# Half tiles of a routed MLP behind pooled attention: split weights fetched from DRAM, choices made earlier, and a new table of issue times

## The chip, the cores and the metric

The kernel runs on one core of a Trainium2 chip. The metric is the time of one execution on the device in microseconds (us). Before the change the median of three runs is 2346.57 us (2337.69 to 2347.06).

The names used below: PE is the matrix engine (TensorE), ACT the scalar engine, DVE the vector engine, POOL the GpSimd engine, SP the engine whose queue issues most of the transfers. PSUM is the memory that PE writes its sums into, in eight banks.

## The reference

Two stages follow each other. The first is attention in which keys and values are one and the same: `kv` (4 batches of 384 x 32 x 128) is averaged over 4 x 4 blocks, which leaves 768 rows a batch, and multiplied by `w_sr`. Each of the 12288 queries of a batch is scored against them, and the softmax of the scores weighs them.

```python
kv_pool = kv.reshape(B, H // r, r, W // r, r, C).mean(axis=(2, 4))
kv_flat = kv_pool.reshape(B, -1, C) @ w_sr          # keys = values, 768 x 128 a batch
s = scale * (q @ k.transpose(0, 2, 1)); s = s - s.max(-1, keepdims=True)
a = np.exp(s); a /= a.sum(-1, keepdims=True) + 1e-09
x = (a @ v)                                         # 49152 rows of 128
```

The second stage sends each of the 49152 rows to the one of eight experts whose gate logit is largest, runs that expert's two-layer MLP (128 to 1024 to 128, ReLU between) and scales the result by the gate's probability.

```python
expert_idx = np.argmax(x @ w_gate, axis=1)
for e in range(E):
    h = np.maximum(x[mask] @ w1[e], 0.0)
    out[mask] = gate_w[mask, None] * (h @ w2[e])
```

## The kernel before

**Work per tile.** Queries go through in 96 tiles of 512. Every product is made of three matmuls on split numbers: an operand is kept as a high part (a rounding copy, made by ACT) and a low part (the difference, made by POOL or DVE), and `mm3` (L230) adds high x high, high x low and low x high. For a tile of attention, PE computes scores in four groups of 128 queries (`scores`), DVE takes the maxima, ACT the exponentials (`exps`), DVE turns 32 x 32 blocks (`turn_p`), SP moves the blocks with 16 transfers (`move_p`), ACT and POOL split the result in three pieces (`high_p`, `low_p`), and PE multiplies by the values in six steps (`values` 0 to 5, where 0 and 1 read the piece that POOL makes second).

**Routing.** `route` turns the result (`turn_x`, the X matmuls of L500), finds each row's expert and its place among that expert's rows (`places`, L579), and POOL writes the rows into the DRAM buffer `xs` with four indirect transfers (`put`, L595). Before a tile's rows are written, POOL clears the row buffer (`norm`, the memset of L486).

**Expert tiles.** Once an expert has 512 rows, they can be taken. `choose` (L659) picks an expert with a chain of small DVE operations on eight numbers, SP loads the choice into registers (`where`), fetches that expert's split weights from `ws` into one of two buffers (`fetch`, L753, only if the buffer does not hold them yet; 2 MB), and loads the rows (`read`, L723). `experts` then turns the rows (`turn_m`), splits them (`high_m` on ACT, `low_m` on POOL, tile name `xl`), and runs eight pairs of steps: `first(f)` (xh, xl against the first weights), `high_h` on ACT, `low_h` on DVE (tile `hlow`), `second(f)`, which comes a good two steps after its `first`. `turn_y`, `rows_y` (tile `yo`) and POOL's four indirect transfers to the output (`put`, L860) end the tile.

**The end.** 94 expert tiles are of 512 rows. Then at most a few rows are left with each expert, and half tiles of 256 take them: six always (tiles 94 to 99), more behind a branch, which the data here does not take. A half tile before the change loads its expert's unsplit weights (1 MB) into the attention buffers `pb` and `pt` (`fetch_whole`, L759) and splits them in four pieces each with ACT, POOL and DVE (`cut`, L768) into the two weight buffers. Its row numbers `tok` (L805, L809) sit in a pool of three buffers, so that a new one waits until the output transfers of three tiles earlier have landed.

**What sets the order.** Nothing runs in loops: every step is entered into a plan with a time (`at`, L52) and the plan is emitted in order of these times. The times come from the table `AT` (L32), in units of which a tile of 512 has 16. For PE, ACT and DVE the order of emission is the order of issue; POOL and SP take theirs from it too. Each engine works its list off in that order. So a change of numbers in `AT` moves instructions past each other on every engine, and nothing else about them.

**Three further facts used below.** Each batch's keys are pooled by DVE (`pool`, L261) during earlier tiles: three batches of six blocks, so 18 tiles carry an extra reduction. The results of `first` sit in three PSUM banks (`take`, `give`, L180 to L187), so a `first` waits until `low_h` has freed a bank. The scores use one pair of banks in turn.

Of the kernel before, what the change touches and what calls it, by code (L numbers as in the profile page):

```python
# [29 lines left out]


AT = {  # L32
    "turn_q": -0.15, "high_q": 3.34, "low_q": 5.01, "maxima": 1.13, "exps": 2.45, ("first_p", 0): 5.48,
    ("first_p", 1): 4.1, ("first_p", 2): 4.74, ("first_p", 3): 5.1, ("first_p", 4): 5.32,
    ("first_p", 5): 7.4, "first_high": 0.5, "first_low": 1.3, "first_values": 2.69, "turn_p": 2.65,
    "move_p": 17.32, ("high_p", 0): 28.78, ("high_p", 1): 25.01, ("high_p", 2): 29.02, "low_p": 0.45,
    ("values", 0): 37.6, ("values", 1): 38.01, ("values", 2): 39.41, ("values", 3): 39.91,
    ("values", 4): 41.61, ("values", 5): 42.21, "copy_x": 0.6, "turn_x": 1.76, "logits": 0.8, "row": 1.7,
    "gate_exp": 2.27, "gate": 2.29, "ranks": 1.12, "places": 2.13, "put_x": 3.83, "expert": 24.43,
    "fetch": -12.69, "read": -9.0, "weights": -5.6, ("cut", 0, 0): -7.93, ("cut", 1, 0): 3.67,  # L40
    ("cut", 0, 1): 1.14, ("cut", 1, 1): 3.1, "turn_m": -4.57, "high_m": 1.58, "low_m": 2.94, "first": 4.6,
    "high_h": 0.0, "low_h": 1.35, "second": 4.85, "copy_y": 0.52, "pads": 4.0, "split": -14.0, "splits": 11.0, "turn_y": 1.61, "rows_y": 4.66,
}


# [17 lines left out]
def tile_pooled_attention_top1_moe(ctx: ExitStack, tc, q, kv, w_sr, w_gate, w1, w2, out):  # L63
# [154 lines left out]
    def low(dst, src, h, eng=nc.vector):  # L218
        eng.tensor_tensor(out=dst, in0=src, in1=h.bitcast(F32), op=ALU.subtract)  # L219

    def load_turned(name, rows, n):

        blocks = ap.tile([P, T], F32, name=name)
        bv = blocks[:, :n].rearrange("p (t c) -> p t c", c=SQ)
        return blocks, [
            nc.sync.dma_start(out=bv[cs], in_=rows[:, cs].rearrange("(t r) c -> r t c", r=SQ)).ins  # L226
            for cs in (slice(k, k + SQ) for k in range(0, P, SQ))
        ]
# [430 lines left out]
    def choose(j):  # L659
# [26 lines left out]
        if final:  # L686

            less = table("less", E)
            nc.vector.tensor_scalar(
                out=less, in0=rem, scalar1=-1.0, scalar2=float(n), op0=ALU.mult, op1=ALU.add  # L690
            )
            nc.vector.scalar_tensor_tensor(out=less, in0=less, scalar=0.0, in1=pick, op0=ALU.max, op1=ALU.mult)
            nc.vector.tensor_tensor(out=pks[:, 0], in0=pks[:, 0], in1=less, op=ALU.subtract)
            thr = rp.tile([P, 1], F32, name="thr" + tag, bufs=4)
# [28 lines left out]
    def read(j):  # L723
        own = state["tile", j]
        rows = xs[bass.ds(own["row"], size(j)), :]
        own["xb"], gets = load_turned("xb", rows, size(j))
        own["tokf"] = rp.tile([P, G], F32, name="tokf", bufs=3)
        tokf = own["tokf"][:, : size(j) // P]
        gets.append(nc.sync.dma_start(out=tokf, in_=rows[:, P].rearrange("(g p) -> p g", p=P)).ins)
        assert state["sent"] >= min(j + AHEAD, NS - 1)  # L730
        for get in gets:
            for put in state["puts"]:
                tc.add_manual_dep(
                    get, put.name,
                    mybir.DependencyInfo(mybir.DependencyClass.Sync, mybir.DependencyReason.DATA),
                    reason="the rows are there",
                )
            tc.add_to_no_dep_group("rows", get)
        state["puts"] = []

    def weights(t, j):
# [14 lines left out]
                out=wt.bitcast(F32), in_=ws[bass.ds(own["ex"], 1)].rearrange("o p n f -> p (o n) f"), cond=own["new"]  # L756
            )

        def fetch_whole():  # L759
            for n in range(2):  # L760
                own[n] = ap.tile([P, F], F32, name=("pb", "pt")[n])
            nc.sync.dma_start(out=own[0], in_=w1[bass.ds(own["ex"], 1)].rearrange("o p f -> p (o f)"))
            nc.sync.dma_start(
                out=own[1].rearrange("p (f d) -> p f d", d=D),
                in_=w2[bass.ds(own["ex"], 1)].rearrange("o (f p) d -> p (o f) d", p=P),
            )
# [6 lines left out]
        at(t + AT["fetch"], where)  # L773
        if j < FULL:
            at(t + AT["weights"], fetch)
            return
        at(t + AT["fetch"], fetch_whole)
        for n in range(2):
            for c in range(F // T):
                at(t + AT["cut", n, c], cut, n, c)  # L780

    def experts(t, j):
        own = {}
        wt = wts[j % 2]
        n = size(j)
        per = T // n

# [9 lines left out]
        def low_m():  # L797
            own["xl"] = mp.tile([P, T], F32R, name="xl")[:, :n]
            low(own["xl"], own["xt"], own["xh"], nc.gpsimd)
            gs = slice(0, n // P)  # L800
            tok = own["tok"] = rp.tile([P, G], I32, name="tok", bufs=3)
            if own["thr"] is None:
                nc.gpsimd.tensor_copy(out=tok[:, gs], in_=own["tokf"][:, gs])
            else:
                old = rp.tile([P, G], F32, name="old")  # L805
                nc.vector.tensor_scalar(
                    out=old[:, gs], in0=slot[:, gs], scalar1=own["thr"], scalar2=BIG, op0=ALU.is_lt, op1=ALU.mult
                )
                nc.vector.tensor_tensor(out=tok[:, gs], in0=old[:, gs], in1=own["tokf"][:, gs], op=ALU.add)  # L809

        def first(f):
            if state.pop("head", False):
                scores_in(0)
                free.append(5)
            hp = own["hp", f] = take()
            for k in range(per):
                fs = slice((f * per + k) * P, (f * per + k + 1) * P)
                mm3(hp[:, k * n : (k + 1) * n], wt[:, 0, fs], wt[:, 1, fs], own["xh"], own["xl"], True, True)
# [12 lines left out]

        def second(f):
            y = own["y"] = ps[:, BANK_Y, :n]
            for k in range(per):
                fb, ns = f * per + k, slice(k * n, (k + 1) * n)
                fs = slice(fb * D, (fb + 1) * D)
                mm3(
                    y, wt[:, 2, fs], wt[:, 3, fs], own["hh", f][:, ns], own["hl", f][:, ns],
                    fb == 0, fb == FB - 1,
                )  # L840

# [44 lines left out]
    def tiles(i, u):  # L886

        if i >= AHEAD:
            tile_j(i - AHEAD, u)

    def tile_j(j, u=None):
        t = 16 * (min(j, FULL) + AHEAD + 3) + 8 * max(j - FULL, 0) + AT["expert"]
# [55 lines left out]
```

## Time and profile before

| | us |
|---|---|
| median of three runs | 2346.57 |
| the profiled execution | 2344.68 |
| its span in the trace | 2343.0 |
| PE busy | 2179.0 (93% of the span) |
| POOL busy | 1832.5 (78%) |
| DVE busy | 1777.1 (76%) |
| ACT busy | 1494.3 (64%) |

The span is what the trace covers, first to last instruction; 1.7 us of the execution lie outside it. The granted clock of PE is its full 2.4 GHz for nearly the whole span, and lower in the first 200 us and in the last 80. PE's busy time counts matmuls that overlap in its pipeline. POOL's busy time leaves out the 0.3 us between two indirect transfers, so its 78% understates how full its queue is. The time line has three parts: a start of about 200 us in which the attention runs ahead, a long steady part in which one attention tile and one expert tile go through together, and an end of about 120 us with expert tiles alone.

### The profile page before, as it was taken

To read this page: it belongs to the slowest core of one execution; us is meant where nothing else is said; L and a number is where in the kernel's file an instruction comes from. 1 tells how busy PE (TensorE), PEld (TensorE's weight loads), DVE (VectorE), ACT (ScalarE), POOL (GpSimd) and SP (SyncE) were. 2 spreads that over 40 slices of the span, in tenths; PEclk is the share of its full clock that TensorE was granted. 3 is DMA by queue.
4 is the path that set the end of the run, shared out by engine and by line. 5 is a ranking of instruction groups with operands and counts; after the bars stand their busy time and mean duration, and the time that the engine had idled before them with its cause. 6 is when DMAs were issued, how large, how long until landed. Compare 5 with 4: busy or idle time off the path is not lost.

```text
span 2343.0 us, 41042 instructions
## 1 busy us (share of the span) xinstructions
PE 2179.0 (93%) x10630; PEld 1788.3 (76%) x10630; DVE 1777.1 (76%) x4368; ACT 1494.3 (64%) x3031; POOL 1832.5 (78%) x1957
## 2 busy tenths in 40 slices
PE   6778999999999999999999999999998999999986
PEld 6667877778777787778877777777786878788765
DVE  2566878987777778987786778998776777877564
ACT  2656666666666676666666666666665666666553
POOL 2656888878887888878887888878887888888863
PEclk9999999999999999999999999999999999999997
DMA  8866556655565556655556556665556555554341
GB/s 237 282 191 148 124 133 157 161 122 116 121 156 145 125 116 157 160 139 117 119 143 159 127 119 147 163 146 123 113 151 143 128 119 119 127 119 112 89 116 53
DMA packets 590357, 324.59 MB, mean 139 GB/s; under 512 B 497048, under 2 KB 515609, under 8 KB 588064
## 3 DMA queue, kind: packets, MB, share of 16 engines
q1 hardware_dynamic: 565408, 268.34, 51.0%
q0 software_dynamic: 24704, 53.53, 6.6%
q8 instruction: 87, 1.43, 0.3%
q14 instruction: 158, 1.29, 0.2%
HBM read 287.84 MB, written 72.88 MB: 154 GB/s over the span
## 4 chain that ended last, share of the span: by engine, by line
POOL 31%; PE 21%; DMA 13%; issue 13%; DVE 9%; SPq 8%; ACT 3%; POOLq 0%; DVEq 0%; ACTq 0%
POOL pt L219 18%; PE ps L231 7%; PE ps L232 6%; DMA xs<-row,dst 6%; PE ps L233 6%; POOL out_dram L860 5%; DMA xb<-xs 5%; POOL xs L595 4%; SPq L382 4%; SPq L226 3%; DVE hlow L826 3%; ACT prob L362 2%; POOL pos L586 1%; PE ps L500 1%; DVE pb L371 1%
## 5 line engine op out<-in xcount | busy, mean ns | idle before, releaser
L822 ACT ACTIVATE hh<-ps 128x512 fp32r<-128x512 f32 x776 | 465.3, 600 | 323.4 <-PE ps L233 309.8
L826 DVE SCALAR_TENSOR_TENSOR hlow<-ps,hh 128x512 fp32r<-128x512 f32 x776 | 529.1, 682 | 179.7 <-ACT hh L822 177.8
L219 POOL TENSOR_TENSOR pt<-pt,pth 128x1024 fp32r<-128x1024 f32 x270 | 640.4, 2413 | 2.8 <-ACT pth L216 1.8
L362 ACT ACTIVATE prob<-ps,nmax 128x768 f32<-128x768 f32 x384 | 346.2, 902 | 265.4 <-DVE nmax L354 265.2
L860 POOL DMA_INDIRECT out_dram<-yo,tok x388 | 384.8, 992 | 130.1 <-issue 79.9
L595 POOL DMA_INDIRECT xs<-row,dst x384 | 380.1, 990 | 116.1 <-issue 89.4
L371 DVE STREAM_TRANSPOSE pb<-prob 128x768 f32<-128x768 f32 x360 | 352.1, 978 | 88.5 <-ACT prob L362 78.6
L231 PE MATMUL ps<-xh,wt 128*128 128x512 f32 (+1 forms) x800 | 340.3, 425 | 75.2 <-DVE hlow L826 64.3
L354 DVE TENSOR_REDUCE nmax<-ps 128x1 f32<-128x768 f32 x384 | 364.7, 950 | 51.2 <-PE ps L233 49.9
L231 PE MATMUL ps<-hh,wt 128*128 128x512 f32 (+1 forms) x800 | 323.2, 404 | 0.0
L216 ACT CAST pth<-pt 128x1024 fp32r<-128x1024 f32 x270 | 273.4, 1047 | 69.6 <-DMA pt<-pb 55.2
L232 PE MATMUL ps<-hlow,wt 128*128 128x512 f32 (+1 forms) x800 | 314.1, 393 | 2.7 <-DVE hlow L826 2.7
L232 PE MATMUL ps<-xl,wt 128*128 128x512 f32 (+1 forms) x800 | 314.1, 393 | 1.5 <-POOL xl L219 1.5
L233 PE MATMUL ps<-xh,wt 128*128 128x512 f32 (+1 forms) x800 | 313.7, 392 | 0.0
L233 PE MATMUL ps<-hh,wt 128*128 128x512 f32 (+1 forms) x800 | 312.1, 390 | 0.0
L231 PE MATMUL ps<-kh,qh 128*128 128x384 f32 x768 | 269.7, 351 | 4.6 <-ACT qh L216 2.3
L232 PE MATMUL ps<-kl,qh 128*128 128x384 f32 x768 | 260.4, 339 | 0.0
L233 PE MATMUL ps<-kh,ql 128*128 128x384 f32 x768 | 259.6, 338 | 0.8 <-POOL ql L219 0.8
L231 PEld LDWEIGHTS ps<-xh,wt 128*128 128x128 f32 x800 | 153.4, 192 | 118.2 <-DVE hlow L826 95.1
L232 PE MATMUL ps<-pt,vh 128*128 128x512 f32 x540 | 213.8, 396 | 3.4 <-POOL pt L219 3.4
L231 PE MATMUL ps<-pth,vh 128*128 128x512 f32 x540 | 214.6, 397 | 0.0
L233 PE MATMUL ps<-pth,vl 128*128 128x512 f32 x540 | 213.8, 396 | 0.0
(133 smaller groups left out, 3824.6 us busy)
## 6 DMA issues: line engine op xcount, KB each, us to landing
wt<-ws SPq DMA_DIRECT2D x94, 2048.0 KB
pt<-pb SPq DMA_DIRECT2D x1440, 96.0 KB
raw<-in_kv_dram SPq DMA_DIRECT2D x96, 256.0 KB
qb<-in_q_dram SPq DMA_DIRECT2D x384, 64.0 KB
xb<-xs SPq DMA_DIRECT2D x376, 64.0 KB
ws<-wt SPq DMA_DIRECT2D x8, 2048.0 KB
raw<-in_moe_w_dram SPq DMA_DIRECT2D x16, 512.0 KB
out_dram<-yo,tok POOLq DMA_INDIRECT x388, 2.3
```

The source lines that it names most:

```text
L216: nc.scalar.copy(out=dst, in_=src)
L219: eng.tensor_tensor(out=dst, in0=src, in1=h.bitcast(F32), op=ALU.subtract)
L231: nc.tensor.matmul(out=ps, lhsT=wh, rhs=xh, start=start, stop=False)
L232: nc.tensor.matmul(out=ps, lhsT=wh, rhs=xl, start=False, stop=False)
L233: nc.tensor.matmul(out=ps, lhsT=wl, rhs=xh, start=False, stop=stop)
L354: nc.vector.tensor_reduce(out=nmax, in_=own["s", g][:, :, :NH], op=ALU.max, axis=AX.XY, negate=True)
L362: nc.scalar.activation(out=prob.rearrange("p (h k) -> p h k", h=2), in_=own["s", g][:, :, :NH], func=AF.Exp, bias=own["nmax", g], scale=1. ...
L371: nc.vector.transpose(out=own["pb"][:, :, :, g, :].rearrange("p c b t -> p b c t"), in_=own["prob", g].rearrange("p (b c t) -> p b c t", c ...
L595: put = nc.gpsimd.indirect_dma_start(out=xs, out_offset=bass.IndirectOffsetOnAxis(ap=dst[:, g : g + 1].bitcast(U32), axis=0), in_=own["row ...
L822: nc.scalar.activation(out=hh, in_=own["hp", f], func=AF.Relu)
L826: nc.vector.scalar_tensor_tensor(out=hl, in0=own["hp", f], scalar=0.0, in1=own["hh", f].bitcast(F32), op0=ALU.max, op1=ALU.subtract,)
L860: put = nc.gpsimd.indirect_dma_start(out=out, out_offset=bass.IndirectOffsetOnAxis(ap=own["tok"][:, g : g + 1].bitcast(U32), axis=0), in_= ...
```

## The change

Five things change.

1. The half tiles take the split weights from `ws`, 2 MB each, without a condition and in two transfers of 1 MB. The fetches go into four sets of buffers in turn: two sets are the buffers of `pb` and `pt`, two are the weight buffers of the full tiles. `cut` and its splits are gone.
2. The half tiles' rows go into buffers of the names `raw` and `prob`, which the attention no longer needs by then.
3. The choices of the experts for tiles 94 to 99 are planned one after the other, 4.6 units apart, right behind that of tile 93; before, each was planned 6 units ahead of its `where`.
4. The pools of `tok`, `tokf` and `thr` get eight buffers and that of `num` four; `old` moves to PSUM.
5. The table `AT` has other numbers in some 30 entries, so that the order on every engine is another.

```diff
-    "turn_q": -0.15, "high_q": 3.34, "low_q": 5.01, ...
+    "turn_q": 0.06, "high_q": 3.87, "low_q": 5.01, ...
...
-    def load_turned(name, rows, n):
-        blocks = ap.tile([P, T], F32, name=name)
+    def load_turned(name, rows, n, pool=ap):
+        blocks = pool.tile([P, T], F32, name=name, bufs=3 if name in ("raw", "prob") else 2)
...
-        num = rp.tile([P, 3], I32, name="num" + tag)
+        num = rp.tile([P, 3], I32, name="num" + tag, bufs=4)
...
-        own["xb"], gets = load_turned("xb", rows, size(j))
-        own["tokf"] = rp.tile([P, G], F32, name="tokf", bufs=3)
+        k = (j - FULL) % 6
+        own["xb"], gets = load_turned(*(("xb", rows, size(j)) if j < FULL else
+                                        ("raw", rows, size(j), kp) if k < 3 else ("prob", rows, size(j))))
+        own["tokf"] = rp.tile([P, G], F32, name="tokf", bufs=8)
...
-        def fetch_whole():
-            for n in range(2):
-                own[n] = ap.tile([P, F], F32, name=("pb", "pt")[n])
-            nc.sync.dma_start(out=own[0], in_=w1[bass.ds(own["ex"], 1)].rearrange("o p f -> p (o f)"))
...
-        def cut(n, c):
-            cs = slice(c * T, (c + 1) * T)
-            high(wt[:, 2 * n, cs], own[n][:, cs])
-            low(wt[:, 2 * n + 1, cs], own[n][:, cs], wt[:, 2 * n, cs], nc.vector if c else nc.gpsimd)
+        def fetch_end():
+            k = (j - FULL) % 4
+            if k < 2:
+                w1p = ap.tile([P, 2, F], F32, name="pb").bitcast(F32R)
+                w2p = ap.tile([P, 2, F], F32R, name="pt")
+            else:
+                w1p, w2p = wts[j % 2][:, :2], wts[j % 2][:, 2:]
+            own["wt"] = (w1p, w2p)
+            for n, w in enumerate(own["wt"]):
+                nc.sync.dma_start(
+                    out=w.bitcast(F32),
+                    in_=ws[bass.ds(own["ex"], 1)].rearrange("o p n f -> p (o n) f")[:, 2 * n : 2 * n + 2],
+                )
...
+        u = start(j - 4) + (size(j - 4) // 32 - 2) + AT["first"] + AT["second"] + 0.1
+        u = t + AT["fetch_end"] if j < FULL + 2 else max(t + AT["fetch_end"], u)
+        at(t + AT["fetch_end"], where)
+        at(u, fetch_end)
...
-            tok = own["tok"] = rp.tile([P, G], I32, name="tok", bufs=3)
+            tok = own["tok"] = rp.tile([P, G], I32, name="tok", bufs=8)
...
-                old = rp.tile([P, G], F32, name="old")
+                old = table("old", G)
...
-        if ("tile", j) not in state:
-            select(t + AT["fetch"] - 6 if u is None else u, j)
+        t = start(j)
+        if j < SURE:
+            state["chosen"] = state["chosen"] + 4.6 if u is None else u
+        if j != SURE:
+            select(state["chosen"] if j < SURE else t + AT["fetch_end"] - 6, j)
         weights(t, j)
-        at(t + AT["read"], read, j)
+        at(t + AT["read"] if j < FULL else t + AT["fetch_end"] + 0.1, read, j)
```

What the new table does to the order is seen at three places. The first is POOL's queue over one period of the steady part. Names: `pt` and `pth` are the pieces of `low_p`, `pos` and `dst` the places, `xs` the routed rows, `out_dram` the output, `row` the buffer that the memset clears. Before:

```order
L860 DMA out_dram<-yo,tok 49152x128 x4
L219 TENSOR_TENSOR pt<-pt,pth 128x4x256 x3
L586 TENSOR_TENSOR pos<-pos,oh 128x8 x3
L587 TENSOR_TENSOR pos<-pos,oh 128x32
L219 TENSOR_TENSOR ql<-qt,qh 128x512
L803 CAST tok<-tokf 128x4
L595 DMA xs<-row,dst 397312x144 x4
L219 TENSOR_TENSOR xl<-xt,xh 128x512
L486 MEMSET row 128x4x15
L487 TENSOR_SCALAR row<-slot 128x4
```

POOL's queue in the same period, after the change:

```order
L219 TENSOR_TENSOR pt<-pt,pth 128x4x256 x3
L586 TENSOR_TENSOR pos<-pos,oh 128x8 x3
L587 TENSOR_TENSOR pos<-pos,oh 128x32
L219 TENSOR_TENSOR ql<-qt,qh 128x512
L595 DMA xs<-row,dst 397312x144 x4
L868 DMA out_dram<-yo,tok 49152x128 x4
L219 TENSOR_TENSOR xl<-xt,xh 128x512
L809 CAST tok<-tokf 128x4
L486 MEMSET row 128x4x15
L487 TENSOR_SCALAR row<-slot 128x4
```

The four output transfers have moved from behind the memset to right behind the four row transfers, ahead of `xl` and of the memset.

The second place is PE in the same part, from the turning of a finished expert tile (`ident,yt`) on. `xh` marks a `first`, `hh` a `second`, `vh` a step of `values`, `kh,qh` scores. Before:

```order
L849 MATMUL ps<-ident,yt 128x128 x4
L231 MATMUL ps<-xh,wt_109 128x512
L232 MATMUL ps<-xl,wt_109 128x512
L233 MATMUL ps<-xh,wt_109 128x512
L273 MATMUL ps<-ident,pooled 128x128
L231 MATMUL ps<-hh,wt_109 128x512
L232 MATMUL ps<-hlow,wt_109 128x512
L233 MATMUL ps<-hh,wt_109 128x512
L231 MATMUL ps<-kh,qh 128x384
```

PE at that place after the change:

```order
L857 MATMUL ps<-ident,yt 128x128 x4
L231 MATMUL ps<-xh,wt_109 128x512
L232 MATMUL ps<-xl,wt_109 128x512
L233 MATMUL ps<-xh,wt_109 128x512
L273 MATMUL ps<-ident,pooled 128x128
L231 MATMUL ps<-pth,vh 128x512
L232 MATMUL ps<-pt,vh 128x512
L233 MATMUL ps<-pth,vl 128x512
L231 MATMUL ps<-hh,wt_109 128x512
L232 MATMUL ps<-hlow,wt_109 128x512
L233 MATMUL ps<-hh,wt_109 128x512
L231 MATMUL ps<-kh,qh 128x384
```

`values` 0 has moved ahead of a `second`, of six score matmuls and of the `first` behind them. (This period is one with a block of keys, hence L273; the others read the same without it.)

The third place is POOL at the end of the program, from the last `pos` on. Before:

```order
L586 TENSOR_TENSOR pos<-pos,oh 128x8 x3
L587 TENSOR_TENSOR pos<-pos,oh 128x32
L803 CAST tok<-tokf 128x4
L595 DMA xs<-row,dst 397312x144 x4
L219 TENSOR_TENSOR xl<-xt,xh 128x512
L860 DMA out_dram<-yo,tok 49152x128 x4
L803 CAST tok<-tokf 128x4
L219 TENSOR_TENSOR xl<-xt,xh 128x512
L860 DMA out_dram<-yo,tok 49152x128 x4
L219 TENSOR_TENSOR wt_109<-pb,wt_109 128x512
L219 TENSOR_TENSOR xl<-xt,xh 128x256
```

POOL at the end after the change:

```order
L586 TENSOR_TENSOR pos<-pos,oh 128x8 x3
L587 TENSOR_TENSOR pos<-pos,oh 128x32
L809 CAST tok<-tokf 128x4
L595 DMA xs<-row,dst 397312x144 x4
L868 DMA out_dram<-yo,tok 49152x128 x4
L219 TENSOR_TENSOR xl<-xt,xh 128x512
L868 DMA out_dram<-yo,tok 49152x128 x4
L809 CAST tok<-tokf 128x4
L219 TENSOR_TENSOR xl<-xt,xh 128x512
L868 DMA out_dram<-yo,tok 49152x128 x4
L219 TENSOR_TENSOR xl<-xt,xh 128x256 x2
```

Here too four output transfers stand ahead of the `xl` that used to precede them, and the splits of the weights (`wt`) are gone.

## Rows read from the trace of the kernel before

**Rows 1.** Instructions by source line, copy_x: durations in ns, first and last start us.
```profile
L430 ACT COPY xt<-ps x90: 577/586/588, 208.6 to 2223.7; 128x512 f32<-128x512 f32 x90
```

**Rows 2.** Windows of one period each: us, busy us by engine, clock, DMA share, GB/s.
```profile
1829.83:1851.45 21.62, 21.44 (x105) 17.75 (x104) 17.38 (x44) 15.00 (x31) 18.22 (x18) 1.00 0.55 124
2028.77:2050.90 22.13, 21.70 (x105) 17.67 (x104) 17.81 (x44) 14.99 (x30) 18.92 (x20) 1.00 0.54 121
983.65:1007.25 23.60, 22.40 (x110) 18.35 (x109) 21.43 (x49) 15.59 (x34) 19.35 (x22) 1.00 0.65 157
1754.77:1781.51 26.74, 21.77 (x103) 17.33 (x102) 17.89 (x44) 14.89 (x32) 18.85 (x20) 1.00 0.77 213
```

**Rows 3.** Waits from 280 to 2200 us: us in total, times, longest us.
```profile
POOL row L486 <- DMA xs<-row,dst: 90.0, 68, 5.6
...
PE ps L231 <- DMA wt<-ws: 4.1, 2, 2.4
```

**Rows 4.** Timeline of POOL, one period: start us, us; idle before and releaser in brackets.
```profile
2093.29 1.31 POOL L219 TENSOR_TENSOR xl<-xt,xh 128x512 fp32r<-128x512 f32 x1
2095.22 0.15 POOL L486 MEMSET row<- 128x60 f32 x1 [0.62 <-DMA xs<-row,dst]
...
2096.03 1.06 POOL L860 DMA_INDIRECT out_dram<-yo,tok  x1 [0.47 <-ACT xt L430]
...
2100.93 7.11 POOL L219 TENSOR_TENSOR pt<-pt,pth 128x1024 fp32r<-128x1024 f32 x3
```

**Rows 5.** Timeline of POOL, PE and ACT in a later period.
```profile
2144.72 7.12 POOL L219 TENSOR_TENSOR pt<-pt,pth 128x1024 fp32r<-128x1024 f32 x3
...
2152.00 0.39 PE L232 MATMUL ps<-pt,vh 128*128 128x512 f32 x1
...
2156.40 0.58 ACT L855 COPY yo<-ps 128x512 f32<-128x512 f32 x1
...
2158.33 0.97 POOL L595 DMA_INDIRECT xs<-row,dst  x1 [0.30 <-issue]
...
2159.32 1.32 POOL L219 TENSOR_TENSOR xl<-xt,xh 128x512 fp32r<-128x512 f32 x1
...
2165.60 0.39 PE L232 MATMUL ps<-xl,wt 128*128 128x512 f32 x1
```

**Rows 6.** Timeline of PE and POOL in periods with a block of keys.
```profile
1021.12 0.51 PE L231 MATMUL ps<-xh,wt 128*128 128x512 f32 x1 [0.86 <-DVE hlow L826]
...
1027.23 0.15 POOL L486 MEMSET row<- 128x60 f32 x1 [1.75 <-DMA xs<-row,dst]
```

**Rows 7.** Timeline of SP and PE around a fetch of new weights.
```profile
1750.44 0.37 SPq L755 DMA_DIRECT2D wt<-ws  x1
...
1760.07 0.47 PE L231 MATMUL ps<-xh,wt 128*128 128x512 f32 x1 [2.43 <-DMA wt<-ws]
```

**Rows 8.** Waits from 2264 us to the end.
```profile
DVE tok L809 <- DMA out_dram<-yo,tok: 19.5, 4, 6.1
...
PE ps L231 <- DVE hlow L826: 16.8, 5, 5.9
```

**Rows 9.** Window of the half tiles, columns as in rows 2.
```profile
2264.85:2343.00 78.15, 48.76 (x311) 46.33 (x309) 38.19 (x110) 31.32 (x65) 34.46 (x34) 0.80 0.28 75
```

**Rows 10.** Timeline of the end, PE and ACT.
```profile
2240.26 0.50 PE L232 MATMUL ps<-xl,wt 128*128 128x512 f32 x1 [1.50 <-POOL xl L219]
...
2264.85 0.28 PE L231 MATMUL ps<-xh,wt 128*128 128x256 f32 x1
...
2278.54 0.28 PE L232 MATMUL ps<-xl,wt 128*128 128x256 f32 x1
2278.66 0.28 PE L233 MATMUL ps<-xh,wt 128*128 128x256 f32 x1
...
2294.96 0.38 PE L849 MATMUL ps<-ident,yt 128*128 128x128 f32 x2
...
2332.77 0.37 ACT L844 COPY yt<-ps 128x256 f32<-128x256 f32 x1 [1.48 <-PE ps L233]
```

More of the change, by code (lines that the diff above doesn't have):

```diff
@@ L32 @@
 AT = {
[L33 to L42, printed above, removed]
+    "turn_q": 0.06, "high_q": 3.87, "low_q": 5.01, "maxima": 1.13, "exps": 2.45, ("first_p", 0): 6.3,
+    ("first_p", 1): 4.35, ("first_p", 2): 4.74, ("first_p", 3): 4.29, ("first_p", 4): 5.32,
+    ("first_p", 5): 7.4, "first_high": 0.5, "first_low": 1.3, "first_values": 2.69, "turn_p": 2.92,
+    "move_p": 17.32, ("high_p", 0): 28.78, ("high_p", 1): 25.01, ("high_p", 2): 29.02, "low_p": 0.53,
+    ("values", 0): 35.64, ("values", 1): 37.68, ("values", 2): 39.08, ("values", 3): 38.39,
+    ("values", 4): 41.28, ("values", 5): 41.88, "copy_x": 0.6, "turn_x": 2.27, "logits": 0.8, "row": 1.7,
+    "gate_exp": 2.27, "gate": 2.29, "ranks": 1.12, "places": 1.32, "put_x": 3.83, "expert": 24.43,
+    "fetch": -12.69, "read": -9.0, "weights": -5.6, "turn_m": -2.09, "high_m": 1.16, "low_m": 2.94, "first": 4.6,
+    "high_h": 1.2, "low_h": 1.35, "second": 4.85, "fetch_end": -26.0, "copy_y": 0.52, "pads": 4.0, "split": -12.61,
+    "splits": 10.92, "turn_y": 1.61, "rows_y": 4.66,
 }
@@ L693, in choose @@
             nc.vector.tensor_tensor(out=pks[:, 0], in0=pks[:, 0], in1=less, op=ALU.subtract)
-            thr = rp.tile([P, 1], F32, name="thr" + tag, bufs=4)
+            thr = rp.tile([P, 1], F32, name="thr" + tag, bufs=8)
             nc.vector.reduce_sum(out=thr, in_=less, axis=AX.X)
             yield
-        num = rp.tile([P, 3], I32, name="num" + tag)
+        num = rp.tile([P, 3], I32, name="num" + tag, bufs=4)
         with nc.allow_low_precision("row numbers below 2**24 are exact"):
@@ L757, in fetch @@
             )
-        def fetch_whole():
-            for n in range(2):
-                own[n] = ap.tile([P, F], F32, name=("pb", "pt")[n])
-            nc.sync.dma_start(out=own[0], in_=w1[bass.ds(own["ex"], 1)].rearrange("o p f -> p (o f)"))
[L763 to L766, printed above, removed]
-        def cut(n, c):
-            cs = slice(c * T, (c + 1) * T)
-            high(wt[:, 2 * n, cs], own[n][:, cs])
-            low(wt[:, 2 * n + 1, cs], own[n][:, cs], wt[:, 2 * n, cs], nc.vector if c else nc.gpsimd)
-        at(t + AT["fetch"], where)
+        def fetch_end():
[11 more added lines that the diff above has]
+                )
+        state["wt", j] = own
         if j < FULL:
+            own["wt"] = (wt[:, :2], wt[:, 2:])
+            at(t + AT["fetch"], where)
             at(t + AT["weights"], fetch)
             return
[L777 to L780, printed above, removed]
+        u = start(j - 4) + (size(j - 4) // 32 - 2) + AT["first"] + AT["second"] + 0.1
+        u = t + AT["fetch_end"] if j < FULL + 2 else max(t + AT["fetch_end"], u)
+        at(t + AT["fetch_end"], where)
+        at(u, fetch_end)
     def experts(t, j):
         own = {}
-        wt = wts[j % 2]
         n = size(j)
@@ L815, in first @@
             hp = own["hp", f] = take()
+            wt = state["wt", j]["wt"][0]
             for k in range(per):
@@ L833, in second @@
             y = own["y"] = ps[:, BANK_Y, :n]
+            wt = state["wt", j]["wt"][1]
             for k in range(per):
@@ L837, in second @@
                 mm3(
-                    y, wt[:, 2, fs], wt[:, 3, fs], own["hh", f][:, ns], own["hl", f][:, ns],
+                    y, wt[:, 0, fs], wt[:, 1, fs], own["hh", f][:, ns], own["hl", f][:, ns],
                     fb == 0, fb == FB - 1,
@@ L889, in tiles, with start @@
             tile_j(i - AHEAD, u)
+    def start(j):
+        return 16 * (min(j, FULL) + AHEAD + 3) + 8 * max(j - FULL, 0) + AT["expert"]
     def tile_j(j, u=None):
-        t = 16 * (min(j, FULL) + AHEAD + 3) + 8 * max(j - FULL, 0) + AT["expert"]
-        if ("tile", j) not in state:
-            select(t + AT["fetch"] - 6 if u is None else u, j)
+        t = start(j)
[3 more added lines that the diff above has]
+            select(state["chosen"] if j < SURE else t + AT["fetch_end"] - 6, j)
         weights(t, j)
-        at(t + AT["read"], read, j)
+        at(t + AT["read"] if j < FULL else t + AT["fetch_end"] + 0.1, read, j)
         experts(t, j)
```

## The prediction, made before the changed kernel was run

> **What bounds the kernel now.** First I split the time line by the source-line view: `copy_x` runs once a tile, so its first and last start count periods [rows 1]. From 208.6 to 2223.7 us there are 89 of them in 2015.1 us. The windows of single periods [rows 2] then show three kinds. The quickest last 21.62 us with PE busy for 21.44: PE's own floor. A period with a block of keys lasts 23.60, with PE busy 22.40 and DVE 21.43. A passage in which an expert's weights change lasts 26.74. Eighteen key periods (three batches, six blocks) are 18 x 23.60 = 424.8; the other 71 share 1590.3, a mean of 22.40. They lie 0.78 above the floor, 55 us in all.
>
> Next I looked for who causes these 55 us. The waits of the steady part [rows 3] name one big entry that isn't a mere echo of PE: POOL's clearing of `row` waits for the row transfers (`xs`), 68 times, 90.0 us, at most 5.6. POOL's timeline [rows 4] shows why: the memset comes right behind the transfers that read the same buffer, with only `xl` (1.31) between, so POOL stands until they land. POOL can't afford it. Its busy 18.22 [rows 2] leaves out 0.30 us ahead of each of eight indirect transfers [rows 5], 2.4 us, which makes 20.6 of 21.62; a wait over 1 us lengthens the period, and 90.0/68 = 1.3 is the mean. In a key period the wait is about 1.75 [rows 6], 31.5 us for eighteen, but there PE and DVE are as late, so it costs nothing. This leaves 58.5 us of wait against 55 us of excess. POOL's wait sets the period outside key periods.
>
> The last 78.15 us [rows 9] hold 48.76 of PE work at a clock of 0.80. There the chain goes through DVE: `tok` waits for the output transfers of three tiles earlier, 19.5 us in four waits, and PE in turn for DVE's `hlow`, 16.8 in five [rows 8].
>
> **Steady part: output transfers ahead of `xl` and the memset.** Four transfers take 2096.03 to 2100.93 = 4.90 us [rows 4]. Moved to right behind the row transfers, they, `xl` (1.3) and a small cast (0.2) put some 6.4 us between the last `xs` transfer and the memset, where 1.3 and a gap stood. The longest wait was 5.6 [rows 3], so the wait goes. POOL's work stays as it is.
>
> What is late next? Three handovers get tight. (a) `xl` comes four transfers later, 4.9 + 0.3 = 5.2 at most; before, it ended at 2159.32 + 1.32 = 2160.64 and PE used it at 2165.60 [rows 5], a slack of 4.96. It is short by about 0.2. (b) `values` 0 moves ahead of a `second`, six score matmuls and a `first`: its second matmul, at 2152.00 in rows 5, would come some 2.45 earlier (two groups of three full matmuls, each twice the half-size spacing of 0.12 [rows 10], are 1.4; six score matmuls of three quarters that size 1.05), at 2149.55. The piece it reads is the second of three from 2144.72 on, so ready at 2144.72 + 4.75 = 2149.47 [rows 5]. Just in time. (c) The output transfers now start at 2158.33 + 0.97 + 0.30 = 2159.60, and `yo`, which they send, is done at 2156.40 + 0.58 = 2156.98 [rows 5]: 2.6 us to spare. The shortfall of (a) is settled once, since PE may fall some tenths behind POOL in a period and stay so; it isn't paid each time. So PE's floor of 21.62 comes next, and the bound of the gain is 55.
>
> I don't take all of it. New weights still cost: they are issued at 1750.44 and PE starts on them at 1760.07, 9.63 us later, having waited 2.43 [rows 7]. Three such passages, of two periods each, hold about 4 us each that POOL's wait doesn't explain: 12 us stay. Rows 2 also show a common period of 22.13 with PE at 21.70, so a few tenths stay here and there. I take **-40** (bounds -55 and 0).
>
> **Key periods.** The moved `values` 0 gives PE something to do where it waits 0.86 for `hlow` [rows 6]. DVE, busy 21.43 of 23.60, keeps its amount. I take -0.5 for each of 18, **-9** (bounds -13 and 0).
>
> **The end.** What the six half tiles need if nothing waits: PE's spacing of half-size matmuls is 0.12 [rows 10], 48 matmuls a tile are 5.76, with 0.3 to 0.4 for turning the rows, 6.1 a tile, 36.7 for six. Ahead of them 2.7 remain of the full tile, behind them 0.7 until the last sum is ready and 2343.0 - 2332.77 = 10.2 from the last `yt` to the end [rows 10]. Together 50.3, against 78.15: -27.9 at best. This is what the end gives if both kinds of waits vanish: eight buffers for `tok` take away the wait for landed output; the splits leave ACT, POOL and DVE, which then make `hh` and `hlow` at once.
>
> Three things come back. First, `xl` of the last tiles now stands behind four transfers on POOL. There PE already waited 1.50 for `xl` [rows 10], no slack at all, so about 5.4 is added once: +5.4. Second, during such a wait of 7 us the clock may fall; of rows 9 (0.80 over the stretch) I take +2. Third, the weights. A half tile fetches 2 MB where it fetched 1. A fetch into reused buffers is issued when the tile four earlier ends. By the row, 2 MB took at most 9.63 us from issue to use [rows 7], beside other loads; at 6.1 us a tile the last three fetches, issued from the end of tile 93 on, land after 9.6, 19.2 and 28.8, and tile 99 needs its at about 27.6: +1.2. Sum -27.9 + 5.4 + 2 + 1.2 = **-19** (bounds -28 and 0, the latter if the loads go on at half the speed of the row).
>
> A rule speaks to the third. The Trainium skill, "DMA: Bandwidth & Descriptors", section Specifications, puts the HBM limit of a core at about 358 GB/s; 2.1 MB would be an estimate of 5.9 us, under the 6.1 of a half tile, and the +1.2 would go. The row's 9.63 us, in a window that moved 213 GB/s [rows 2], doesn't reach that rate.
>
> **The start.** Other positions of the first splits and of the first values: 0, within 6 to either side; the waits there are spread over all engines and no row singles one out.
>
> **Sum.** -40 - 9 - 19 = -68 on the profiled execution's 2344.68 (span 2343.0 and 1.7 outside): 2276.7, taken as 2276. The median of the three runs is 1.9 above that execution, which I let go in the rounding of the steady part.
>
> **Rivals.** *Another wait takes the place of POOL's.* The tight handovers (a) and (b) have slacks of -0.2 and +0.1, so PE could wait for `xl` or `pt` each period as long as POOL waited before. For it: POOL's queue is as full as PE's. Against it: POOL would need 22.4 us of work and has 20.6. Then only the end and a little of the key periods gain: 2344.7 - 21 = 2324.
>
> *The end gives nothing.* The half tiles become bound by 2 MB each at the 9.63 us of rows 7 or worse, with `xl` on top: six such are 58, with 5.4 of `xl`, 2.7 ahead and 10.9 behind 77, as before. Only the steady part gains: 2344.7 - 49 = 2296.
>
> *Slower.* ACT and DVE work in order, and `xh` and the turning of the rows (`turn_m`) now stand ahead of `hh` and `hlow`; output transfers that wait for `yo` hold `xl` behind them on POOL. If `yo` slips past its 2.6 us of room, as it is nearest to do in key periods, POOL stands with five things queued, PE waits for `xl`, and `yo`, which needs PE, slips again: a circle in which each period pays. At 0.8 us more than the 22.40 of now, 71 periods are +57; with the end's -21 the time is 2381. It decides from about 0.3 us a period on, where it eats what the end gives. Against it: the 2.6 us that `yo` has to spare are four passes of ACT over such a tile at 0.58 [rows 5], and only one or two move ahead of it.
>
> *It doesn't do what it says.* POOL's wait only moves: the rows land as late as the next thing POOL waits for, and the period stays, while the end loses in `xl` what it wins in `tok`: about 2344.
>
> **How the numbers follow.** My forecast 0.62, with a range of its own from 2250 to 2297; the other wait 0.15; the end without gain 0.11; no change 0.06; slower 0.06. Half a per cent, 12 us, is about what a measurement of this kernel can tell from no change. The first three cases lie below that: faster 0.88, same 0.06, slower 0.06. The range: the low end takes the full -55 - 13 - 28 and rounds to 2245; the high end reaches to the other-wait case, 2326. Outside are the two last cases and a little of the tails.
>
> **What would show it.** Right: POOL's wait for `xs` at the memset is gone from the waits; a common period is 21.6 to 21.8 and a key period about 23.1; in the last 120 us PE waits once for POOL's `xl`, about 7 us; DVE no longer waits at `tok`; half tiles follow at about 6.1 us, and PE's wait for weights there is 3 us at most. Wrong: PE waiting every period for `xl`, `pt` or `hlow`; POOL's output transfers waiting for ACT's `yo`; half tiles 8 us or more apart with PE waiting for weights.

## The result, and the profile after

The changed kernel takes 2317.35 us (median of four runs, 2308.98 to 2323.7) against 2345.83 of the kernel before: a ratio of 0.9886, with a 95% interval from 0.9866 to 0.9905. That is a gain of 28 us, in the range but less than half of the 68 forecast. The profiled execution took 2322.58 us, with a span of 2320.8.

The starts of `copy_x` [rows 1] cut both time lines into four parts. They add up to the spans; "key periods" are the seven of each of the three batches that hold its six blocks of keys and what follows the last.

| us | before | forecast | after | change |
|---|---|---|---|---|
| start, to the first `copy_x` of the steady part | 208.6 | 0 | 206.4 | -2.2 |
| 68 periods without a block of keys | 1524.1 (22.41 each) | -40 | 1466.3 (21.56) | -57.8 |
| 21 key periods | 491.1 (23.39 each) | -9 | 535.2 (25.48) | +44.1 |
| from the last `copy_x` to the end | 119.3 | -19 | 112.9 | -6.4 |

`copy_x` in the changed kernel, by source line (first and last start at the end):

```profile
L430 ACT COPY xt<-ps x90: 577/588/591, 206.4 to 2207.9; 128x512 f32<-128x512 f32 x90
```

Three windows of the changed kernel, with the columns of [rows 2]: a common period, a common key period, and the first key period of the second batch.

```profile
2020.21:2041.53 21.32, 21.32 (x105) 17.82 (x104) 17.24 (x44) 15.19 (x31) 18.74 (x21) 1.00 0.56 126
975.11:998.84 23.73, 22.41 (x110) 18.25 (x109) 21.25 (x49) 15.99 (x34) 18.83 (x21) 1.00 0.66 157
895.98:926.76 30.78, 24.35 (x110) 20.15 (x109) 29.42 (x49) 16.10 (x33) 17.87 (x22) 0.89 0.52 118
```

The common period is shorter than the 21.62 that I had taken for PE's floor, with PE busy throughout. In the last row DVE is busy for 29.42 us with the same 49 instructions that take 21.25 in the row above: one of them has grown by 8 us, and no idle time of DVE shows it. The waits from 280 to 2200 us, which answer to [rows 3]:

```profile
POOL row L486 <- DMA xs<-row,dst: 35.8, 20, 2.7
...
PE ps L232 <- POOL xl L219: 25.1, 20, 3.0
PE ps L231 <- DVE hlow L833: 25.1, 4, 6.4
...
PE ps L231 <- DMA wt<-ws: 9.9, 6, 2.6
```

POOL's wait at the memset fell from 90.0 to 35.8. PE now waits 20 times for `xl`, which it did not before; 18 of these waits, 22.7 us, lie in key periods. For `hlow` at L231 it waits four times, some 6.3 us each; in the kernel before these waits were many and short:

```profile
PE ps L231 <- DVE hlow L826: 44.3, 56, 2.5
```

One of the four, on DVE first:

```profile
897.25 0.96 DVE L371 STREAM_TRANSPOSE pb<-prob 128x768 f32<-128x768 f32 x1
898.12 8.36 DVE L269 TENSOR_TENSOR pooled<-half 128x128 f32<-128x128 f32 x1
906.41 0.68 DVE L833 SCALAR_TENSOR_TENSOR hlow<-ps,hh 128x512 fp32r<-128x512 f32 x1
```

On POOL and on PE at the same time:

```profile
897.68 1.32 POOL L219 TENSOR_TENSOR xl<-xt,xh 128x512 fp32r<-128x512 f32 x1
898.90 0.22 POOL L809 CAST tok<-tokf 128x4 int32<-128x4 f32 x1
...
899.36 6.97 POOL L219 TENSOR_TENSOR pt<-pt,pth 128x1024 fp32r<-128x1024 f32 x3
...
907.14 0.80 PE L231 MATMUL ps<-xh,wt 128*128 128x512 f32 x1 [6.43 <-DVE hlow L833]
```

L269 (`join`) adds the two halves of a pooled key block, 128 x 128 numbers. It takes 0.25 us as a rule; here 8.36, from 898.12 to 906.48, just as long as POOL's run of `xl`, cast, memset and `low_p` lasts (to 906.33). Behind PE's wait of 6.43 us the granted clock is at its lower level (1.2 GHz) for 5 us, and matmuls of 512 columns start 0.43 us apart instead of 0.23:

```profile
907.00:912.00 5.00, 4.86 (x13) 4.28 (x14) 4.72 (x17) 2.97 (x9) 0.00 (x0) 0.51 0.06 15
```

Behind the other three waits 5 us have a clock of 0.50 to 0.64. The view of the addition's source line shows all 18 with minimum, median and maximum in ns; four took 8.33 to 9.13 us:

```profile
L269 DVE TENSOR_TENSOR pooled<-half x18: 241/251/9135, 359.2 to 1578.7; 128x128 f32<-128x128 f32 x18
```

In the kernel before all 18 start beside output transfers and none is long. One of them, with POOL's rows around it:

```profile
914.85 0.27 DVE L269 TENSOR_TENSOR pooled<-half 128x128 f32<-128x128 f32 x1
...
915.35 0.97 POOL L860 DMA_INDIRECT out_dram<-yo,tok  x1 [0.30 <-DMA xb<-xs]
916.63 0.97 POOL L860 DMA_INDIRECT out_dram<-yo,tok  x1 [0.30 <-issue]
917.60 2.42 POOL L219 TENSOR_TENSOR pt<-pt,pth 128x1024 fp32r<-128x1024 f32 x1
```

There the addition comes 2.75 us ahead of POOL's long run. In the changed kernel the output transfers have moved ahead of `xl` and `xl`, memset and `low_p` follow one another (in most key periods the memset comes before those transfers, and `xl`, cast and `low_p` are the run), so the addition lies close to the start of the run.

At the end, the waits from 2207 us on:

```profile
POOL out_dram L868 <- ACT yo L863: 31.6, 8, 10.5
...
PE ps L232 <- POOL xl L219: 17.4, 5, 6.2
```

DVE's wait at `tok` [rows 8] is gone, and PE's waits for `hlow`, 16.8 us in five, have shrunk to 0.9 in two. Half tiles follow each other at 5.96 us, as the starts of `yt` show:

```profile
2288.49 0.37 ACT L852 COPY yt<-ps 128x256 f32<-128x256 f32 x1
2294.47 0.37 ACT L852 COPY yt<-ps 128x256 f32<-128x256 f32 x1
2300.41 0.38 ACT L852 COPY yt<-ps 128x256 f32<-128x256 f32 x1
```

But PE waits five times for `xl`. POOL's queue shows why:

```profile
2245.63 0.99 POOL L868 DMA_INDIRECT out_dram<-yo,tok  x1 [10.51 <-ACT yo L863]
...
2252.41 1.27 POOL L219 TENSOR_TENSOR xl<-xt,xh 128x512 fp32r<-128x512 f32 x1
```

POOL stands 10.51 us at an output transfer for `yo`, with the next tile's `xl` queued behind it.

### The profile page after: what moved, and what is told of

Its sections match the earlier page's. It is cut to its first block, busy times and chain, and to the rows that moved or that the text cites. A ratio compares the mean times of both kernels' runs of the same rounds, so it can differ in the third digit from the quotient of the medians.

```text
span 2320.8 us, 40858 instructions
## 1 busy us (share of the span) xinstructions
PE 2174.4 (94%) x10630; PEld 1806.5 (78%) x10630; DVE 1783.0 (77%) x4356; ACT 1495.2 (64%) x3007; POOL 1808.2 (78%) x1945
## 5 line engine op out<-in xcount | busy, mean ns | idle before, releaser
L868 POOL DMA_INDIRECT out_dram<-yo,tok x388 | 379.2, 977 | 168.7 <-issue 88.0
L231 PE MATMUL ps<-xh,wt 128*128 128x512 f32 (+1 forms) x768 | 325.0, 423 | 39.4 <-DVE hlow L833 26.0
L231 PE MATMUL ps<-hh,wt 128*128 128x512 f32 (+1 forms) x768 | 321.7, 419 | 0.0
L232 PE MATMUL ps<-hlow,wt 128*128 128x512 f32 (+1 forms) x768 | 306.1, 399 | 0.0
L233 PE MATMUL ps<-xh,wt 128*128 128x512 f32 (+1 forms) x768 | 305.0, 397 | 0.0
L233 PE MATMUL ps<-hh,wt 128*128 128x512 f32 (+1 forms) x768 | 303.4, 395 | 0.0
L231 PE MATMUL ps<-kh,qh 128*128 128x384 f32 x768 | 266.0, 346 | 6.0 <-ACT prob L362 3.7
L231 PE MATMUL ps<-pth,vh 128*128 128x512 f32 x540 | 215.6, 399 | 0.0
L232 PEld LDWEIGHTS ps<-xl,wt 128*128 128x128 f32 x768 | 147.2, 192 | 65.5 <-POOL xl L219 50.7
```

Source lines behind the costliest of these rows:

```text
L231: nc.tensor.matmul(out=ps, lhsT=wh, rhs=xh, start=start, stop=False)
L232: nc.tensor.matmul(out=ps, lhsT=wh, rhs=xl, start=False, stop=False)
L233: nc.tensor.matmul(out=ps, lhsT=wl, rhs=xh, start=False, stop=stop)
L868: put = nc.gpsimd.indirect_dma_start(out=out, out_offset=bass.IndirectOffsetOnAxis(ap=own["tok"][:, g : g + 1].bitcast(U32), axis=0), in_= ...
```

## The experiments

All medians in us; the ratio is to the kernel before on the same chip (2338.7 to 2340.2 there, some 6 us below the 2345.83 above). The four parts are read as above.

| run | median | ratio (95%) | start | per period, no keys | per key period | end |
|---|---|---|---|---|---|---|
| e1 half in PSUM | 2286.95 | 0.9781 (0.9762 to 0.9801) | 206.8 | 21.57 | 23.80 | 109.5 |
| e2 join late | 2447.08 | 1.0462 (1.0440 to 1.0485) | 209.5 | 22.33 | 28.49 | 119.7 |
| e3 three row buffers | 2337.52 | 0.9990 (0.9980 to 1.0001) | 211.4 | 22.32 | 23.37 | 117.4 |
| e4 end only | 2318.87 | 0.9918 (0.9900 to 0.9936) | 208.7 | 22.36 | 23.43 | 95.3 |
| e5 = e1, values old | 2345.54 | 1.0031 (1.0020 to 1.0042) | 205.1 | 22.72 | 22.87 | 109.4 |
| e6 = e1, turn_m old | 2253.70 | 0.9638 (0.9620 to 0.9657) | 207.7 | 21.54 | 23.13 | 95.1 |
| e7 = e1, xl on VectorE | 2271.23 | 0.9713 (0.9693 to 0.9733) | 206.9 | 21.59 | 23.93 | 92.4 |
| e8 before, rows on ACT | 2404.80 | 1.0288 (1.0269 to 1.0307) | 198.0 | 21.82 | 28.57 | 119.0 |
| e9 = e8, half in PSUM | 2291.17 | 0.9792 (0.9776 to 0.9808) | 198.4 | 21.77 | 23.38 | 119.3 |
| e10 = e6, rows on ACT | 2241.94 | 0.9582 (0.9566 to 0.9598) | 198.6 | 21.47 | 23.15 | 93.8 |
| e11 = e6, xl on VectorE | 2251.33 | 0.9619 (0.9603 to 0.9635) | 205.4 | 21.55 | 23.13 | 95.1 |
| e12 before, values new, half in PSUM | 2406.05 | 1.0280 (1.0263 to 1.0297) | 211.2 | 23.30 | 23.48 | 117.9 |

**e1: the addition reads SBUF only once.**

```diff
-            half = own["half", kb, h] = kp.tile([P, C], F32, name="half")
+            half = own["half", kb, h] = table("half", P, 1) if h else kp.tile([P, C], F32, name="half")
```

> The changed kernel, with one of the two halves of a key block written to PSUM, so that the addition that joins them (L269 on VectorE) reads SBUF only once; the order on every engine is the same. Theory (the addition, with two operands in SBUF, stands until GpSimd's run of SBUF operations ends: four of 18 took 8.3 to 9.1 us): all 18 additions take under 0.5 us, the four PE waits of 6.4 us for hlow go, and the time falls by 25 to 36 us, to some 2285. Rival (the addition waits for its data, a late load or reduction): four additions of 8 us stay and the time stays near 2317.

Measured: 2286.95 us, and no addition over 0.26 us:

```profile
L269 DVE TENSOR_TENSOR pooled<-half,ps x18: 238/252/259, 358.9 to 1549.5; 128x128 f32<-128x128 f32 x18
```

Key periods fall from 25.48 to 23.80 us, 35.4 us in all; the other parts stay, but for 3.4 us at the end. (By the ratios, 0.9886 and 0.9781, the medians lie some 25 us apart; the profiled execution of the changed kernel took 5 us more than its median.) Three of the additions start 0.46 to 0.48 us into `xl`, as two of the four long ones did in the changed kernel (0.44 and 0.48), and are not held up:

```profile
894.19 1.31 POOL L219 TENSOR_TENSOR xl<-xt,xh 128x512 fp32r<-128x512 f32 x1
...
894.66 0.24 DVE L269 TENSOR_TENSOR pooled<-half,ps 128x128 f32<-128x128 f32 x1
```

The place of the second operand alone decides, with the order on every engine the same. The rival falls.

**e2: the same addition placed into POOL's run.**

```diff
-                at(u + 0.7 * step, join, kb)
+                at(u + 0.7 * step + 3.2, join, kb)
```

> The kernel before, with that addition moved a few places back in VectorE's order, so that it starts while GpSimd runs low_p (7.1 us). Theory of the blocked port: each of the 18 additions takes 3 to 7 us instead of 0.25, and the time rises by 40 to 110 us. Rival of late data: later is safer, 0.25 us each, the time stays at 2346.

Measured: 2447.08 us, 108 more, with all 18 additions long:

```profile
L269 DVE TENSOR_TENSOR pooled<-half x18: 5031/5881/7343, 370.0 to 1682.1; 128x128 f32<-128x128 f32 x18
```

Key periods take 5.1 us more and nothing else changes. So the kernel before was open to this too; its order only kept the two apart.

**e3: three row buffers before.**

```diff
-            row = own["row"] = rp.tile([P, G, W], F32, name="row")
+            row = own["row"] = rp.tile([P, G, W], F32, name="row", bufs=3)
```

> The kernel before with three row buffers instead of two, nothing else: the memset no longer waits for the transfers just issued. Theory of the prediction (this wait sets the period outside key periods): the 90 us of wait go, those periods fall from 22.40 to about 21.4 us, the time by 45 to 65 us. Rival (the new order on PE, values 0 earlier, brought the gain): periods stay above 22 and the time falls by less than 15.

Measured: 2337.52 us, no change, but the wait did not go:

```profile
POOL row L486 <- DMA xs<-row,dst: 81.7, 63, 5.1
```

With a third buffer free, the memset moved one tile ahead in POOL's list and stood right behind the transfers that read its new buffer, as before. The run decides nothing; e8 and e9 take the wait away in another way.

**e4: the new end with the old table.**

```diff
-    "turn_q": 0.06, "high_q": 3.87, ...
+    "turn_q": -0.15, "high_q": 3.34, ...
```

> The changed kernel's code with the table of the kernel before: only the end is new. Theory (the end's own gain of 23 us is spent again because xl stands behind the output transfers at five tiles): with the old table the full tiles at the end keep their pace and the time falls by 15 to 25 us, to about 2325. Rival (the end as coded is worth only some 6 us, as the two profiles show): about 2340.

Measured: 2318.87 us, 20 less than before, and the end falls from 119.3 to 95.3. The code of the end is worth 24 us; with the new table it was 6.4.

**e5: values at their old times.**

```diff
-    ("values", 0): 35.64, ("values", 1): 37.68, ("values", 2): 39.08, ("values", 3): 38.39,
-    ("values", 4): 41.28, ("values", 5): 41.88, ...
+    ("values", 0): 37.6, ("values", 1): 38.01, ("values", 2): 39.41, ("values", 3): 39.91,
+    ("values", 4): 41.61, ("values", 5): 42.21, ...
```

> The changed kernel with one half in PSUM (as e1, 2287 us, which is what it is compared with), and with the six entries for values of the kernel before; GpSimd's order stays the new one (output transfers, xl, memset). Theory (outside key periods GpSimd's order, which takes the memset's wait away, brought the gain of 58 us): those periods stay at 21.5 to 21.8 us and the time at 2280 to 2297. Rival (values earlier on TensorE brought it): they go back to 22.3 and the time to about 2335.

Measured: 2345.54 us; periods without keys go to 22.72, though POOL keeps the new order. The waits from 280 to 2200 us:

```profile
POOL xs L595 <- DVE ps L647: 87.9, 83, 1.5
...
PE ps L232 <- POOL xl L219: 55.3, 60, 2.6
```

With later values the routing is later, POOL's row transfers wait for DVE in 83 periods, the output transfers and `xl` behind them come later, and PE waits for `xl` in 60. My theory (POOL's order alone) falls: POOL's wait at the memset is nearly gone in this run (0.9 us), so it isn't that wait that holds the periods. `xl` behind the transfers can be afforded only where the values come early.

**e6: rows turned at their old time.** GpSimd then has `xl` ahead of the output transfers and the memset behind them.

```diff
-    ... "turn_m": -2.09, "high_m": 1.16, ...
+    ... "turn_m": -4.57, "high_m": 1.58, ...
```

> As e1, with the entries turn_m and high_m of the kernel before: on GpSimd xl stands ahead of the output transfers again, in the whole program, and the memset still behind them. Theory (xl behind four transfers costs the end 14 us and key periods some 0.4 us each, and gives nothing; the gain is the memset's place): periods outside key blocks stay at 21.6, the stretch from the last copy_x to the end falls from 109.5 to 95 to 98 us, the time to 2262 to 2272. Rival (rows turned later on ACT and VectorE are part of the gain): those periods rise by 0.3 or more, and the time is 2285 or more.

Measured: 2253.70 us, better than expected. Periods without keys stay at 21.54, key periods fall to 23.13, the end to 95.1. In the last 95 us one wait for `xl` is left:

```profile
PE ps L232 <- POOL xl L219: 1.1, 1, 1.1
```

**e7: xl at the end on another engine.**

```diff
-            low(own["xl"], own["xt"], own["xh"], nc.gpsimd)
+            low(own["xl"], own["xt"], own["xh"], nc.vector if j >= FULL - 3 else nc.gpsimd)
```

> As e1, with xl of the last nine tiles made by VectorE instead of GpSimd, so that no output transfer stands ahead of it. Theory (PE's five waits for xl, 17 us, are what the end lost): the end falls from 109.5 to 93 to 99 us, the time to about 2274. Rival (the clock and the choices of experts hold the full tiles at the end): end above 104, the time above 2281.

Measured: 2271.23 us, the end 92.4 instead of 109.5. In e1 PE's five waits for `xl` there come to:

```profile
PE ps L232 <- POOL xl L219: 15.7, 5, 6.2
```

In e7 0.2 of them is left, while waits for `hlow` grow from 0.9 to 4.3: 12 us net. The other 5 of the 17.1 are the clock. From the last `copy_x` to the end it is 0.89 in e1 and 0.96 in e7, and PE is busy for 83.4 us there against 78.1 for the same matmuls.

**e8: POOL without memset and wait, in the kernel before.**

```diff
+    rowbuf = [cp.tile([P, G, W], F32, name=f"row{n}") for n in range(2)]
...
-            row = own["row"] = rp.tile([P, G, W], F32, name="row")
-            nc.gpsimd.memset(row[:, :, P + 1 :], 0.0)
-            nc.gpsimd.tensor_scalar(
...
+        def number():
+            row = own["row"] = rowbuf[i % 2]
+            nc.scalar.copy(out=row[:, :, P], in_=ids[:, i * G : (i + 1) * G])
...
+        at(t - 1, number)
```

> The kernel before, where ACT writes the row numbers into two fixed row buffers seven units later, and the other columns are cleared once; GpSimd has neither the memset nor its wait. (With three buffers, e3, the memset only moved a tile ahead and waited as long as before.) Theory (the wait sets the periods outside key blocks): they fall from 22.41 to 21.7 or less, the time by 45 to 65 us. Rival (PE's and VectorE's order sets them, POOL's wait is slack): above 22.1, the time falls by less than 20.

Measured: 2404.80 us, slower where 45 to 65 us less were expected. Periods without keys fall from 22.41 to 21.82, nearly as far as expected, but key periods rise to 28.57: POOL, no longer waiting, begins its run earlier and meets the addition in every one of them.

```profile
L269 DVE TENSOR_TENSOR pooled<-half x18: 6186/6669/7521, 352.3 to 1647.1; 128x128 f32<-128x128 f32 x18
```

**e9: the same, with e1's edit.**

> e8 again (the kernel before without the memset and its wait on GpSimd), with one half of a key block in PSUM, so that the blocked additions of e8 (18 of 6.2 to 7.5 us) go. Theory (the wait for the row buffers was worth some 0.6 us a period outside key blocks, and nothing else in e8 is changed): those periods stay at 21.8 us, key periods come back to 23.0 to 23.6, the time is 2290 to 2302. Rival (GpSimd's or ACT's new order costs key periods by itself): key periods above 24.5, the time above 2320.

Measured: 2291.17 us, 21.77 and 23.38 us per period, as the theory had it. POOL's wait, with the 0.4 us of memset and row numbers that left POOL together with it, was worth (22.41 - 21.77) x 68 = 44 us; the start, which I had not thought of, gave another 10.

**e10: e6 with e8's edit.**

> e6 (the fastest so far, 2254 us) with the row numbers written by ACT into fixed buffers, as in e8: GpSimd has 0.4 us a period less to do and no wait for rows (13 us in all in e6). Theory (outside key blocks GpSimd's queue, full without a gap at 21.3 us, sets the period): it falls from 21.54 to 21.2 or less, the time to 2225 to 2242. Rival (TensorE's own work sets it there): 21.4 to 21.6, the time within 8 us of 2254.

Measured: 2241.94 us. The theory falls: periods without keys went from 21.54 to 21.47 only; of the 14 us between the two profiled spans 9 come from the start. Windows from 1795 to 2095 us of e10, then of e6:

```profile
1795.00:2095.00 300.00, 299.76 (x1465) 250.53 (x1464) 243.26 (x608) 213.06 (x436) 260.17 (x253) 1.00 0.55 124
```

```profile
1795.00:2095.00 300.00, 299.83 (x1463) 250.30 (x1462) 241.96 (x604) 211.09 (x421) 264.80 (x282) 1.00 0.56 125
```

PE is busy for all of the 300 us in both, while POOL got 4.6 us less to do. TensorE's own work is the bound there, at about 21.3 us a period.

**e11: e6 with e7's edit.**

> e6 with xl of the last nine tiles made by VectorE. With the output transfers already behind xl there is little to win: the end from 95.1 to 92 to 95 us, the time within 4 us of 2254. Rival (GpSimd's queue still holds xl at the end, behind the transfers of the tile before): the end below 90.

Measured: 2251.33 us, the end unchanged at 95.1: nothing is left to win by `xl` there. The 2.4 us between the medians are no effect of the edit that a part shows: the profiled starts differ by 2.3 us (207.7 and 205.4), and the edit doesn't touch the start.

**e12: only the values new, in the kernel before with e1's edit** (e5's diff the other way round).

> The kernel before with the half in PSUM and the six entries for values of the changed kernel, nothing else; on GpSimd the memset then stands right behind the row transfers and its wait stays. Theory (values earlier makes the routing come earlier, and the memset's wait has to go too: each alone brings part): periods outside key blocks 21.9 to 22.3, the time 2310 to 2335. Rival (values earlier is the whole gain): 21.6 or less, the time below 2295. Rival (it is nothing without the new place of the transfers): 22.4 or more.

Measured: 2406.05 us, with 23.30 us per period without keys: the last rival holds, and the change alone even loses. In POOL's list the memset now stands right behind the row transfers, and its wait doubles:

```profile
POOL row L486 <- DMA xs<-row,dst: 172.3, 81, 6.3
```

So neither the early values with the memset's wait (23.30) nor the late `xl` with old values (22.72) gains. With the wait gone, early values give 21.5, be `xl` late (e1) or early (e6), and old values with an early `xl` give 21.77 (e9).

The fastest version is e10, with e6's order, the half in PSUM and the row numbers on ACT: 4.2% less than the kernel before.

## Why the prediction was wrong

**Periods without keys, -40: right in cause, low in size.** POOL's wait at the memset did set them; taken away in the kernel before (e9) it gives 44 us. The measured 57.8 (in 68 periods, where I counted 71) lie beyond my bound of 55, because the 21.62 us of [rows 2] was not PE's floor: that period, too, was still set by others, and PE alone can do 21.3. What I wrote of the moved `values` 0 was one-sided. I counted it as a risk, the second piece just in time. But the change needs the earlier values (all six steps were moved): e5 shows that without them the late `xl` costs PE 55.3 us of waits, and the whole gain. By that run the shortfall of 0.2 in handover (a) was "settled once" only because the routing came earlier as well, a step that I had not followed from the values through `copy_x` to the row transfers.

**Key periods, -9: the step that failed.** "DVE, busy 21.43 of 23.60, keeps its amount", I wrote. Its list did, its time didn't. The sum of 44.1 is 35.4 for the blocked additions (after less e1) and 8.7 for the rest. Of the 35.4, PE's four waits are 25.1, and the lower clock behind them some 9 more, an estimate from its level in the four stretches. The wait for `hlow` that I wanted to fill (16.5 us in the key periods before) did go: in e1 no such wait is left at L231. But 18 waits for `xl` (19.3 us in e1) came in its place: in most key periods the memset still stands ahead of the output transfers and both ahead of `xl`, which the place I looked at, a period without keys, did not show.

```profile
995.75 0.15 POOL L486 MEMSET row<- 128x60 f32 x1 [1.53 <-DMA xs<-row,dst]
...
996.62 1.05 POOL L868 DMA_INDIRECT out_dram<-yo,tok  x1 [0.51 <-ACT pth L216]
...
1002.88 0.49 PE L232 MATMUL ps<-xl,wt 128*128 128x512 f32 x1 [0.70 <-POOL xl L219]
```

With `xl` ahead again (e6) the waits for `xl` are gone from them and key periods come to 23.13, in all 5.4 us under before, where I had forecast 9. (e6 also turns and splits the rows earlier on DVE and ACT, so it is not `xl` alone that moved.)

**The end, -19: two terms mis-sized.** The half tiles came out as worked out (5.96 us apart against 6.1), no weights were waited for (so the +1.2 was not needed), and the code of the end is worth 24 (e4). But I added the wait for `xl` once, 5.4 on top of 1.5; that one measured 6.22, and four more tiles paid 11.2 between them. For the clock I took +2, and the waits cost some 5 by way of it (e7). e7 takes the waits away and gives 17.1, clock included. I had named the mechanism, output transfers waiting for `yo` with `xl` behind them, in the rival that ends slower, for the steady part, where it did not occur; at the end, where PE has no attention tile to go on with, it did.

**The start:** -2.2, within what I had allowed.

**The rivals.** "Another wait takes the place of POOL's" named 2324, close to the time, but for another reason: outside key periods nothing took its place, and in them `xl` took that of `hlow`. None of the four named an instruction on DVE that POOL holds up while it runs.

What stays open: why the start of e8, e9 and e10 is 9 to 11 us shorter (before, POOL waits 14.2 us at the memset there too, in five waits, but no run sets that apart), and whether the changed kernel's spread of 15 us between runs is the number of blocked additions, which only a profile shows; without them (e1) the spread is 5 us.

## What to carry to other kernels

A move on one engine also moves what runs beside it on the others: before GpSimd's operations are packed into one run without waits, look for VectorE instructions with two operands in SBUF that can start in it or close to it. An instruction much longer than its own median may be a wait, even if no view lists it as one. And a wait that goes in the middle is worth what stands behind it in every kind of period; read the new order in each kind, the last tiles too.

## What the runs showed of the hardware

VectorE's addition of two SBUF operands took 5.0 to 9.1 us beside a run of GpSimd (all 18 in e2 and in e8, four in the changed kernel), and 0.25 us with one operand in PSUM (e1, e9). The Trainium skill, "SBUF — State Buffer", section Who interferes with whom, says that such an instruction contends with a GpSimd instruction that reads SBUF, and that the later one blocks until the other is done. The runs agree that it blocks. They go further: it could stand through a whole run of GpSimd instructions (8.36 us, where the first of them took 1.32), and by the profile's starts it lost even when it began a little earlier. The whole run is no rule: one of the 18, which also began inside `xl`, was through in 0.55 us, ahead of `low_p`, which starts at 360.30.

```profile
358.30 1.33 POOL L219 TENSOR_TENSOR xl<-xt,xh 128x512 fp32r<-128x512 f32 x1
...
359.24 0.55 DVE L269 TENSOR_TENSOR pooled<-half 128x128 f32<-128x128 f32 x1
```

Two additions of the changed kernel, one free and one blocked, each with the `xl` behind it:

```profile
1000.84 0.24 DVE L269 TENSOR_TENSOR pooled<-half 128x128 f32<-128x128 f32 x1
...
1001.53 1.29 POOL L219 TENSOR_TENSOR xl<-xt,xh 128x512 fp32r<-128x512 f32 x1
...
1024.60 9.13 DVE L269 TENSOR_TENSOR pooled<-half 128x128 f32<-128x128 f32 x1
...
1025.24 1.29 POOL L219 TENSOR_TENSOR xl<-xt,xh 128x512 fp32r<-128x512 f32 x1
```

0.69 us ahead of `xl` it was free, 0.64 us ahead it took 9.13. Between the two lie 0.05 us, as far as a profile's starts can be read that finely.
